# 64-row tiles for the transposes of q and k, and GpSimd's attention and routing work moved to VectorE and ScalarE

## The chip, the cores and the metric

The kernel runs on one core of one Trainium2 chip. The metric is the device time of one execution in microseconds (us), the median of several runs; lower is better. A core has a matrix engine (PE, with its weight loads listed as PEld), a vector engine (DVE), a scalar engine (ACT), a general engine (GpSimd, listed as POOL) and a queue engine (SP) that issues most of the transfers.

## The reference

Three blocks in a row. The first is a recurrence over time for 4 batches, 8 heads, 768 steps and a head size of 48:

```python
scale = np.minimum(mag, 0.999) / (mag + 1e-06)   # mag = |a_re + i a_im|
for t in range(S):
    new_re = ar * S_re - ai * S_im
    new_im = ar * S_im + ai * S_re
    S_re, S_im = (new_re + kv, new_im)           # kv = outer product of k[t], v[t]
    y[:, :, t] = np.einsum('bhd,bhde->bhe', q[:, :, t], S_re)
```

Its output, 3072 tokens of 384 values, goes through `((x @ w_a) * (x @ w_b)) @ w_out` with 1536 inner columns. The last block sends each token whose skip score `x @ w_skip` is positive to the one of 8 experts with the highest gate value, `relu(x @ w1[e]) @ w2[e]` weighted by the gate's softmax value, and adds the result to the token.

## The kernel before

**Units and groups.** The recurrence is computed in chunks of 128 time steps as a kind of attention. A unit is one chunk of one batch, with all 8 heads side by side in 384 columns; there are 24 units, and two make a group of 256 tokens, 12 groups (`g`). Per unit, `att_exp` makes the magnitudes: logarithms of the decay, a sum over time by a matmul with a triangle (`l2`, with a high and a low part `lh`, `ll` from the fifth unit on), exponentials `t1` and `t2`, and the products `q = q * t1` (line 332) and `k = k * t2` (line 333). The last row of `t1` is turned into a column by a copy `et` of 32 partitions (line 327) and a small transfer. `att_trig` makes the phases: an arctangent, a sum over time (`tp`), rounding (`t3`, line 362), a cosine `t4` and a sine `ts`; the products of q and k with them are `qr` and `kr` (lines 381 and 383), with 96 columns per head.

**The matmuls of a unit** are in `att_pe`. `turned` transposes q and k head by head against the identity (lines 425 and 430), four heads per PSUM bank (`pq`, `pk`), and ACT copies each bank to `tq` or `tk` of 512 columns. `scores` multiplies them in strips of 32 columns of the array (`pcs`, line 444; the first six units do it in whole tiles, `pc`); DVE masks the scores into `sc` (line 453). `delta` (`ds`, line 403) and `y` (line 482) follow, in strips as well. Then `xt` takes over y in a high part on ACT and a low one on DVE (lines 493 and 494), and `new_state` carries the state on (lines 413 and 415).

**The second block**, `moe1`, runs 12 steps per group: 18 matmuls `ab` (lines 615 to 617), an ACT copy `asb`, a DVE product with it (line 623) that frees the bank, `gh` on ACT, `gl` on DVE, and 6 matmuls `op` two steps later (lines 599 to 601). **Routing** of a finished group is `route`: maxima, a one-hot row `oh` from `eq` (lines 681 and 688), running counts `ohs` (line 701), positions, comparisons `sl` of an index row with them (line 738), and a matmul into a table. The experts come after all groups.

**Order.** While group g goes through `moe1`, the attention of group g + 1 and the routing of group g - 2 are worked in between. The order of each engine's instructions up to about the sixth unit is written out by hand (`ORDER`); after that the compiler's list planner chooses it from its own simulated times. Instructions of one engine run in the planned order. PSUM has eight banks: two each for `ab`, `op`, `at` (shared by `l2`, `tp`, `pq`, `pk`, `ds`, `y` and the routing's matmuls, in rotation) and `at2`, which from the seventh unit on hold the scores (`env.pc`). `PLACE` lists units whose operations go to another engine than the usual one.

Of the kernel before, what the change touches and what calls it, by code (L numbers as in the profile page):

```python
# [16 lines left out]
ALU = mybir.AluOpType  # L17
# [62 lines left out]
GF = 5  # L80
WO = DM + 10
# [37 lines left out]
def kern(tc, q, k, v, a_re, a_im, w_a, w_b, w_out, w_skip, w_gate, w1, w2, out):  # L119
# [3 lines left out]
    with st:  # L123
# [167 lines left out]
        def att_exp(i):  # L291
# [23 lines left out]
            if i < SPL:  # L315
                pe.matmul(l2[:, :W], tri, t1, start=True, stop=True)
            else:
                hi, lo = parts(i, "l", ("t3", "t4"))
                copy(on("lh", i, act), hi, t1)
                on("ll", i, pool).tensor_tensor(out=lo, in0=t1, in1=hi, op=ALU.subtract)  # L320
                cumsum(l2, hi, lo)
# [5 lines left out]
            pool.tensor_copy(et[96:], t1[96:].rearrange("p (h d) -> p d h", d=D))  # L327
# [4 lines left out]
            on("q", i, pool).tensor_tensor(out=d["q"], in0=d["q"], in1=t1, op=ALU.mult)  # L332
# [4 lines left out]
        def att_trig(i):  # L337
# [24 lines left out]
            dve.scalar_tensor_tensor(out=t3, in0=t3, scalar=MAGIC, in1=tp[:, :W], op0=ALU.subtract, op1=ALU.subtract)  # L362
# [11 lines left out]
            for nm in ("q", "k"):  # L374
# [8 lines left out]
                ins = e.tensor_tensor(out=r[:, :, 1], in0=src, in1=ts.rearrange("t (h d) -> t h d", d=D), op=ALU.mult)  # L383
                if e is dve:
                    mark((nm + "r", i), ins)
# [4 lines left out]
        def att_pe(i):  # L390
# [3 lines left out]
            sc, qT = [], []  # L394
# [14 lines left out]
            def new_state(ds):  # L409
                s3 = stt.rearrange("p (h e) -> p h e", e=VP)[:, :, :D]  # L410
                d3 = ds[:96, :W].rearrange("p (h e) -> p h e", e=D)
                if c > 0:
                    dve.tensor_tensor(out=s3, in0=s3, in1=d3, op=ALU.add)
                    d3 = s3
                dve.tensor_tensor(out=s3, in0=d3, in1=ee[:, :, None].to_broadcast([96, H, D]), op=ALU.mult)
# [6 lines left out]
            def turned(hh):  # L422
                pq = at(f"pq{i}_{hh}")
                for j in range(4):
                    pe.transpose(pq[:96, j * P : (j + 1) * P], qr[:, 4 * hh + j].rearrange("t x d -> t (x d)"), ident)  # L425
                tq = ew.tile([96, 512], F32, tag="tq", name=f"tq{i}_{hh}", bufs=2)
                mark(("tq", i, hh), copy(on("tq", 2 * i + hh, act), tq, pq[:96]))
                pk = at(f"pk{i}_{hh}")
                for j in range(4):
                    pe.transpose(pk[:96, j * P : (j + 1) * P], kr[:, 4 * hh + j].rearrange("t x d -> t (x d)"), ident)  # L430
                tk = ew.tile([96, 512], F32, tag="tk", name=f"tk{i}_{hh}", bufs=2)
                done = mark(("tk", i, hh), copy(on("tk", 2 * i + hh, act), tk, pk[:96])).ins
                qT.append(tq)
                return tq, tk, done

            def scores(hh, tq, tk, done, last):
                pc = at(f"pc{i}_{hh}") if i < CAUSAL else env.pc[hh]
                for j in range(4):
                    if i < CAUSAL:
                        last = pe.matmul(pc[:, j * P : (j + 1) * P], tk[:, j * P : (j + 1) * P], tq[:, j * P : (j + 1) * P], start=True, stop=True).ins  # L440
                        continue
                    for x in (0, 1, 2, 3) if j % 2 == 0 else (3, 2, 1, 0):
                        y0, p0 = j * P + STRIP * (x if j % 2 == 0 else 3 - x), STRIP * x
                        ins = pe.matmul(pc[p0 : p0 + STRIP, y0 : (j + 1) * P], tk[:, y0 : y0 + STRIP], tq[:, y0 : (j + 1) * P], start=True, stop=True).ins  # L444
# [13 lines left out]
            halves = []  # L458
            for hh in range(2):
                halves.append(turned(hh))  # L460
                if i < CAUSAL:
                    last, msk = scores(hh, *halves[hh], last)
            if i >= CAUSAL:
                for hh in range(2):
                    last, msk = scores(hh, *halves[hh][:2], halves[1][2], last)
# [12 lines left out]
            for s_, inter, h, col, begin, end in (t for row in zip(*strips) for t in row):  # L478
                p0, hh, j = STRIP * (s_ % 4), h // 4, h % 4
                o = y[p0 : p0 + STRIP, s_ // 4 * P : (s_ // 4 + 1) * P]  # L480
                l, r = (stt, qT[hh][:, j * P : (j + 1) * P]) if inter else (vt, sc[hh][:, j])
# [12 lines left out]
            dve.tensor_tensor(out=xt[:, :, 1, us], in0=y3, in1=xt[:, :, 0, us], op=ALU.subtract)  # L494
# [173 lines left out]
        def route(g):  # L668
# [31 lines left out]
            for t in range(2):  # L700
                pool.tensor_tensor(out=ohs, in0=ohs, in1=oh[:, t], op=ALU.add)
# [13 lines left out]
            sls = compare((2 * g, 2 * g + 1), dve if last else pool)  # L715
# [18 lines left out]
        def compare(tiles, eng=pool):  # L734
# [494 lines left out]
```

## Time and profile before

| | |
|---|---|
| median of 3 runs | 845.05 us (844.81 to 845.98) |
| the profiled execution | 847.09 us, of which the span from first to last instruction is 845.4 us |
| mean granted TensorE clock in it | 0.997 |
| busy: PE, DVE, ACT, POOL | 799.0, 559.8, 459.7, 235.0 us |

Busy time is the union of an engine's instructions. Matmuls are pipelined, so the duration of one is longer than its distance to the next, and a busy PE is not one at its peak. Idle time of an engine that sets nothing costs nothing.

### The profile page before, as it was taken

The numbers are of one execution on the slowest core, as the hardware profiler recorded it, in microseconds if no ns is written. First come the engines' busy times: TensorE is split into PE (matmuls) and PEld (weight loads), VectorE is DVE, ScalarE is ACT, GpSimd is POOL, SyncE is SP. The second block draws the span as 40 slices with busy tenths as digits, with TensorE's granted clock in tenths as the row PEclk, the third lists the DMA queues.
The fourth block names the chain that finished last, engine by engine and source line by source line (L and its number), as shares of the span: only waits on it lengthen the run. The fifth ranks groups of instructions, "written<-read, shape, count | busy, mean of one in ns | idle before, by whom it ended". The sixth has DMA issues, their size and how long they took to land.

```text
span 845.4 us, 21833 instructions
## 1 busy us (share of the span) xinstructions
PE 799.0 (95%) x8827; PEld 768.4 (91%) x8827; DVE 559.8 (66%) x1339; ACT 459.7 (54%) x949; POOL 235.0 (28%) x274
## 2 busy tenths in 40 slices
PE   1899999999999999999999999999999999999995
PEld 0589899999999999999999999999999989999995
DVE  7899888695884867738677386673736547555541
ACT  6798655364564655636547365473634325555540
POOL 3131353320311113102130031300304125757650
PEclk9999999999999999999999999999999999999998
DMA  9995223152341522313222132111103239776600
GB/s 256 243 299 131 52 58 77 22 126 38 83 90 25 114 53 72 63 26 85 45 72 58 30 84 45 50 38 28 32 2 115 74 118 347 222 223 199 194 22 23
DMA packets 180959, 83.15 MB, mean 98 GB/s; under 512 B 152084, under 2 KB 168026, under 8 KB 180848
## 3 DMA queue, kind: packets, MB, share of 16 engines
q1 hardware_dynamic: 178800, 76.26, 35.2%
q0 software_dynamic: 2048, 5.40, 1.8%
q8 instruction: 71, 1.16, 0.6%
q14 instruction: 40, 0.33, 0.1%
HBM read 69.84 MB, written 12.61 MB: 98 GB/s over the span
## 4 chain that ended last, share of the span: by engine, by line
PE 80%; DVE 10%; issue 4%; ACT 3%; POOL 1%; DMA 1%; POOLq 0%; ACTq 0%; DVEq 0%
PE ab L615 10%; PE ab L616 10%; PE ab L617 10%; PE op L600 5%; PE op L601 5%; PE op L599 5%; PE y L482 4%; PE eh L901 3%; PE eh L902 3%; PE eh L904 3%; PE eo L918 3%; PE eo L919 3%; PE eo L920 3%; PE pcs L444 2%; PE pq L425 2%
## 5 line engine op out<-in xcount | busy, mean ns | idle before, releaser
L615 PE MATMUL ab<-xt,wa 128*128 128x256 f32 x432 | 124.5, 289 | 7.5 <-DVE asb L623 7.3
L615 PE MATMUL ab<-xt,wb 128*128 128x256 f32 x432 | 123.3, 285 | 0.1
L616 PE MATMUL ab<-xt,wb 128*128 128x256 f32 x432 | 122.8, 284 | 0.0
L617 PE MATMUL ab<-xt,wa 128*128 128x256 f32 x432 | 122.5, 284 | 0.0
L616 PE MATMUL ab<-xt,wa 128*128 128x256 f32 x432 | 122.4, 283 | 0.0
L617 PE MATMUL ab<-xt,wb 128*128 128x256 f32 x432 | 122.2, 283 | 0.0
L623 DVE TENSOR_TENSOR asb<-ab,asb 128x256 f32<-128x256 f32 x144 | 60.3, 419 | 73.0 <-ACT asb L272 71.8
L600 PE MATMUL op<-wo,gh 128*128 128x394 f32 x288 | 99.7, 346 | 1.7 <-POOL wo L512 1.7
L601 PE MATMUL op<-wo,gh 128*128 128x394 f32 x288 | 99.6, 346 | 0.0
L599 PE MATMUL op<-wo,gl 128*128 128x394 f32 x288 | 98.6, 346 | 0.0
L272 ACT ACTIVATE asb<-ab 128x256 f32<-128x256 f32 x139 | 53.0, 381 | 70.1 <-PE ab L617 64.1
L615 PEld LDWEIGHTS ab<-xt,wa 128*128 128x128 f32 x432 | 81.3, 189 | 9.9 <-DVE asb L623 9.1
L272 ACT ACTIVATE gh<-asb 128x256 fp32r<-128x256 f32 x132 | 54.7, 415 | 61.2 <-DVE asb L623 61.2
L616 PEld LDWEIGHTS ab<-xt,wb 128*128 128x128 f32 x432 | 81.4, 188 | 1.3 <-issue 1.2
L617 PEld LDWEIGHTS ab<-xt,wb 128*128 128x128 f32 x432 | 81.3, 188 | 1.1 <-issue 1.0
L615 PEld LDWEIGHTS ab<-xt,wb 128*128 128x128 f32 x432 | 81.4, 188 | 0.9 <-issue 0.6
L616 PEld LDWEIGHTS ab<-xt,wa 128*128 128x128 f32 x432 | 81.4, 189 | 0.7 <-issue 0.4
L617 PEld LDWEIGHTS ab<-xt,wa 128*128 128x128 f32 x432 | 81.3, 188 | 0.0
L627 DVE TENSOR_TENSOR gl<-asb,gh 128x256 fp32r<-128x256 f32 x131 | 60.7, 465 | 30.9 <-ACT gh L272 30.2
L869 POOL TENSOR_TENSOR wq<-stg,wq 128x768 fp32r<-128x768 f32 x32 | 59.5, 1862 | 49.1 <-issue 24.8
L320 POOL TENSOR_TENSOR ll<-t,lh 128x384 fp32r<-128x384 f32 x19 | 19.9, 1050 | 163.1 <-ACT lh L272 118.0
L908 DVE SCALAR_TENSOR_TENSOR hl<-eh,hh 128x256 fp32r<-128x256 f32 x64 | 27.1, 424 | 52.2 <-ACT hh L907 52.1
(257 smaller groups left out, 2123.2 us busy)
## 6 DMA issues: line engine op xcount, KB each, us to landing
stg<-in_moe_w_dram SPq DMA_DIRECT2D x28, 768.0 KB
rawa<-in_moe_w_a_dram SPq DMA_DIRECT2D x6, 768.0 KB
re<-in_a_re_dram SPq DMA_DIRECT2D x24, 192.0 KB
rawb<-in_moe_w_b_dram SPq DMA_DIRECT2D x6, 768.0 KB
q<-in_q_dram SPq DMA_DIRECT2D x24, 192.0 KB
k<-in_k_dram SPq DMA_DIRECT2D x24, 192.0 KB
rawo<-in_moe_w_out_dram SPq DMA_DIRECT2D x6, 768.0 KB
xd<-xr SPq DMA_DIRECT2D x24, 192.0 KB
```

Source lines behind the costliest of these rows:

```text
L272: return act.activation(out=out, in_=in_, func=AF.Copy) if e is act else e.tensor_copy(out, in_)
L482: ins = pe.matmul(o, l[:, col : col + STRIP], r, start=begin, stop=end).ins
L599: pe.matmul(o, gl[:, ts], wh, start=f == 0, stop=False)
L600: pe.matmul(o, gh[:, ts], wl, start=False, stop=False)
L601: i = pe.matmul(o, gh[:, ts], wh, start=False, stop=f == NF - 1)
L615: pe.matmul(o, wl, xt[:, c, 0], start=c == 0, stop=False)
L616: pe.matmul(o, wh, xt[:, c, 1], start=False, stop=False)
L617: pe.matmul(o, wh, xt[:, c, 0], start=False, stop=c == NCC - 1)
L623: dve.tensor_tensor(out=asb, in0=ab[:, 256:], in1=asb, op=ALU.mult)
L627: on("gl", n).tensor_tensor(out=gl, in0=asb, in1=gh, op=ALU.subtract)
L869: lo.tensor_tensor(out=o[:, 1], in0=t, in1=o[:, 0], op=ALU.subtract)
L908: vm = dve.scalar_tensor_tensor(out=gl, in0=o, scalar=0.0, in1=gh, op0=ALU.max, op1=ALU.subtract)
```

## The change

For units 6 to 23 the transposes are cut in halves of 64 rows: each head gives two, one from rows 64 to 127 and one from rows 0 to 63, that take the matching 64 x 64 block of the identity and write 64 columns each, into two banks. All 16 of q and then all 16 of k are tied into one order. q's halves go to two `at` banks, k's to the two score banks. `tq` and `tk` are now single tiles of 1024 columns with one buffer, and each of the four copies writes every second 64 columns. The first transposes wait by hand-made dependencies: for the last product of kr, and in even units for `t3` of the next unit, in odd ones for the low part of `xt` and the first state update of the unit before.

From the ninth unit on (`PORT = 8`), `ll` and the product `q * t1` go to DVE and the copy `et` to ACT; in all groups `ohs` and `sl` go to DVE. In `ORDER` only names of `tq` and `tk` change.

```diff
+PORT = 8
+ROWS = 64
...
-                on("ll", i, pool).tensor_tensor(out=lo, in0=t1, in1=hi, op=ALU.subtract)
+                on("ll", i, pool if i < PORT else dve).tensor_tensor(out=lo, in0=t1, in1=hi, op=ALU.subtract)
...
-            pool.tensor_copy(et[96:], t1[96:].rearrange("p (h d) -> p d h", d=D))
+            copy(pool if i < PORT else act, et[96:], t1[96:].rearrange("p (h d) -> p d h", d=D))
...
-            on("q", i, pool).tensor_tensor(out=d["q"], in0=d["q"], in1=t1, op=ALU.mult)
+            on("q", i, pool if i < PORT else dve).tensor_tensor(out=d["q"], in0=d["q"], in1=t1, op=ALU.mult)
...
-            def turned(hh):
-                pq = at(f"pq{i}_{hh}")
+            tq, tk = (ew.tile([96, H * P], F32, tag=nm, name=f"{nm}{i}", bufs=1) for nm in ("tq", "tk"))
...
+            def turned_rows(nm, dst, r, banks, last):
+                for h in range(H):
+                    for x, p_ in ((1, banks[1]), (0, banks[0])):
+                        rows = slice(ROWS * x, ROWS * (x + 1))
+                        ins = pe.transpose(p_[:96, h * ROWS : (h + 1) * ROWS], r[rows, h].rearrange("t x d -> t (x d)"), ident[rows, rows]).ins
+                        for w in [last] if last else [d["krw"], marks["t3", i + 1]] if i % 2 == 0 else [d["krw"]] + env.free:
+                            after(ins, w, mybir.DependencyClass.NoSync if last else mybir.DependencyClass.Sync)
+                        last = ins
+                d3 = dst.rearrange("e (h t) -> e h t", t=P)
+                for x, p_ in enumerate(banks):
+                    cp = copy(act if x == 0 else act, d3[:, :, ROWS * x : ROWS * (x + 1)], p_[:96].rearrange("e (h t) -> e h t", t=ROWS))
+                return last, cp.ins
...
+            if i < CAUSAL:
                 for hh in range(2):
-                    last, msk = scores(hh, *halves[hh][:2], halves[1][2], last)
+                    turned("q", tq, qr, hh)
+                    turned("k", tk, kr, hh)
+                    last, msk = scores(hh, None, last)
+            else:
+                last, _ = turned_rows("q", tq, qr, [at(f"pq{i}_{x}") for x in range(2)], None)
+                _, done = turned_rows("k", tk, kr, env.pc, last)
+                last = None
+                for hh in range(2):
+                    last, msk = scores(hh, done, last)
...
-            dve.tensor_tensor(out=xt[:, :, 1, us], in0=y3, in1=xt[:, :, 0, us], op=ALU.subtract)
+            env.free = [dve.tensor_tensor(out=xt[:, :, 1, us], in0=y3, in1=xt[:, :, 0, us], op=ALU.subtract).ins]
...
-                pool.tensor_tensor(out=ohs, in0=ohs, in1=oh[:, t], op=ALU.add)
+                dve.tensor_tensor(out=ohs, in0=ohs, in1=oh[:, t], op=ALU.add)
...
-            sls = compare((2 * g, 2 * g + 1), dve if last else pool)
+            sls = compare((2 * g, 2 * g + 1))
...
-        def compare(tiles, eng=pool):
+        def compare(tiles, eng=dve):
```

## Rows read from the trace of the kernel before

**Rows 1.** The page's busy times: us, share of the span, instructions.
```profile
PE 799.0 (95%) x8827; PEld 768.4 (91%) x8827; DVE 559.8 (66%) x1339; ACT 459.7 (54%) x949; POOL 235.0 (28%) x274
```
**Rows 2.** PE's waits, 217 to 640 us: total us, times, longest us.
```profile
PE ab L615 <- DVE asb L623: 6.6, 7, 1.0
```
**Rows 3.** Timeline of PE around a quartet: start, duration in us.
```profile
397.35 0.60 PE L425 MATMUL pq<-ident,qr 128*96 128x128 f32 x4
397.71 0.36 PE L617 MATMUL ab<-xt,wa 128*128 128x256 f32 x1
397.91 0.28 PE L615 MATMUL ab<-xt,wb 128*128 128x256 f32 x1
```
**Rows 4.** Timeline of PE after the y of a unit.
```profile
412.41 0.39 PE L616 MATMUL ab<-xt,wa 128*128 128x256 f32 x1
412.63 0.28 PE L617 MATMUL ab<-xt,wa 128*128 128x256 f32 x1
412.75 0.28 PE L615 MATMUL ab<-xt,wb 128*128 128x256 f32 x1
```
**Rows 5.** Groups of PE, 217 to 539 us: busy us, mean ns, idle before.
```profile
L425 PE MATMUL pq<-ident,qr 128*96 128x128 f32 x96 | 14.4, 272 | 0.0
```
**Rows 6.** Timeline of weight loads, six in a row.
```profile
52.72 0.76 PEld L561 LDWEIGHTS wt<-wg,wtt 128*128 128x128 f32 x6
```
**Rows 7.** Groups of weight loads, whole span.
```profile
L430 PEld LDWEIGHTS pk<-ident,kr 128*96 128x96 f32 x192 | 22.1, 127 | 1.4 <-PE pq L425 0.5
...
L561 PEld LDWEIGHTS wt<-wg,wtt 128*128 128x128 f32 x72 | 9.1, 191 | 1.2 <-ACT wtt L272 1.2
...
L885 PEld LDWEIGHTS xgp<-ident,xg 128*128 128x128 f32 x48 | 5.6, 139 | 0.4 <-DMA xg<-xd,giu 0.4
```
**Rows 8.** Timeline of PE in the ds of a unit.
```profile
409.87 0.26 PE L403 MATMUL ds<-v,kr 128*32 128x48 f32 x6
409.95 0.26 PE L403 MATMUL ds<-u,kr 128*32 128x48 f32 x6
```
**Rows 9.** Groups of DVE by shape, 217 to 540 us.
```profile
L333 DVE TENSOR_TENSOR k<-k,t 128x384 f32<-128x384 f32 x13 | 14.7, 1167 | 11.6 <-ACT t L223 11.6
...
L381 DVE TENSOR_TENSOR kr<-k,t 128x384 f32<-128x384 f32 x12 | 6.6, 549 | 0.0
```
**Rows 10.** Groups of ACT, 217 to 539 us.
```profile
L272 ACT ACTIVATE asb<-ab 128x256 f32<-128x256 f32 x72 | 27.6, 384 | 30.1 <-PE ab L617 27.2 <-PE pt L750 1.6
...
L272 ACT ACTIVATE tq<-pq 96x512 f32<-96x512 f32 x24 | 14.2, 590 | 9.5 <-PE pq L425 9.5
```
**Rows 11.** Groups of POOL, 217 to 539 us.
```profile
L332 POOL TENSOR_TENSOR q<-q,t 128x384 f32<-128x384 f32 x12 | 15.1, 1271 | 0.5
L738 POOL TENSOR_SCALAR sl<-iota,rt_pos 128x256 bf16<-128x256 bf16 x12 | 12.7, 1063 | 0.0
L320 POOL TENSOR_TENSOR ll<-t,lh 128x384 fp32r<-128x384 f32 x12 | 12.6, 1048 | 130.7 <-ACT lh L272 95.7 <-DVE asb L623 35.0
L327 POOL COPY et<-t 32x384 f32<-32x384 f32 x12 | 10.5, 877 | 24.3 <-ACT t L223 23.9
```
**Rows 12.** One tile's instructions (sl): ns min/median/max, first and last start.
```profile
L738 DVE TENSOR_SCALAR sl<-iota,rt_pos x2: 274/298/323, 686.1 to 686.4; 128x256 bf16<-128x256 bf16 x2
```
**Rows 13.** Timeline of all engines at a group's start.
```profile
275.87 0.21 DVE L681 SCALAR_TENSOR_TENSOR eq<-lg,m,desc 128x8 f32<-128x8 f32 x1
...
275.94 0.39 ACT L272 ACTIVATE asb<-ab 128x256 f32<-128x256 f32 x1
...
276.07 0.88 POOL L327 COPY et<-t 32x384 f32<-32x384 f32 x1
...
276.18 0.80 DVE L681 SCALAR_TENSOR_TENSOR eq<-lg,m,desc 128x8 f32<-128x8 f32 x1
...
277.75 0.41 DVE L623 TENSOR_TENSOR asb<-ab,asb 128x256 f32<-128x256 f32 x1
...
278.22 0.39 PE L615 MATMUL ab<-xt,wa 128*128 128x256 f32 x1 [1.00 <-DVE asb L623]
```

More of the change, by code (lines that the diff above doesn't have):

```diff
@@ L361, in att_trig @@
                 dve.tensor_scalar(out=t3, in0=tp[:, :W], scalar1=MAGIC, scalar2=None, op0=ALU.add)
-            dve.scalar_tensor_tensor(out=t3, in0=t3, scalar=MAGIC, in1=tp[:, :W], op0=ALU.subtract, op1=ALU.subtract)
+            marks["t3", i] = dve.scalar_tensor_tensor(out=t3, in0=t3, scalar=MAGIC, in1=tp[:, :W], op0=ALU.subtract, op1=ALU.subtract).ins
             if c + 1 < NCH:
@@ L383, in att_trig @@
                 ins = e.tensor_tensor(out=r[:, :, 1], in0=src, in1=ts.rearrange("t (h d) -> t h d", d=D), op=ALU.mult)
+                d[nm + "rw"] = ins.ins
                 if e is dve:
@@ L393, in att_pe @@
             qr, kr, vt, ee = d["qr"], d["kr"], d["v"], d["ee"]
-            sc, qT = [], []
+            sc = []
             stt = state[b]
@@ L412, in new_state @@
                 if c > 0:
-                    dve.tensor_tensor(out=s3, in0=s3, in1=d3, op=ALU.add)
+                    env.free.append(dve.tensor_tensor(out=s3, in0=s3, in1=d3, op=ALU.add).ins)
                     d3 = s3
@@ L420, in att_pe, with turned @@
             last = None
-            def turned(hh):
-                pq = at(f"pq{i}_{hh}")
+            tq, tk = (ew.tile([96, H * P], F32, tag=nm, name=f"{nm}{i}", bufs=1) for nm in ("tq", "tk"))
+            def turned(nm, dst, r, hh):
+                p_ = at(f"p{nm}{i}_{hh}")
                 for j in range(4):
[L425 to L434, printed above, removed]
@@ L436, in scores @@
-            def scores(hh, tq, tk, done, last):
+                    pe.transpose(p_[:96, j * P : (j + 1) * P], r[:, 4 * hh + j].rearrange("t x d -> t (x d)"), ident)
+                mark(("t" + nm, i, hh), copy(on("t" + nm, 2 * i + hh, act), dst[:, 4 * P * hh : 4 * P * (hh + 1)], p_[:96]))
+            def turned_rows(nm, dst, r, banks, last):
[10 more added lines that the diff above has]
+                return last, cp.ins
@@ L437, in scores @@
+            def scores(hh, done, last):
                 pc = at(f"pc{i}_{hh}") if i < CAUSAL else env.pc[hh]
                 for j in range(4):
+                    tks, tqs = (x[:, (4 * hh + j) * P : (4 * hh + j + 1) * P] for x in (tk, tq))
                     if i < CAUSAL:
-                        last = pe.matmul(pc[:, j * P : (j + 1) * P], tk[:, j * P : (j + 1) * P], tq[:, j * P : (j + 1) * P], start=True, stop=True).ins
+                        last = pe.matmul(pc[:, j * P : (j + 1) * P], tks, tqs, start=True, stop=True).ins
@@ L441, in scores @@
                         continue
                     for x in (0, 1, 2, 3) if j % 2 == 0 else (3, 2, 1, 0):
-                        y0, p0 = j * P + STRIP * (x if j % 2 == 0 else 3 - x), STRIP * x
-                        ins = pe.matmul(pc[p0 : p0 + STRIP, y0 : (j + 1) * P], tk[:, y0 : y0 + STRIP], tq[:, y0 : (j + 1) * P], start=True, stop=True).ins
+                        y0, p0 = STRIP * (x if j % 2 == 0 else 3 - x), STRIP * x
+                        ins = pe.matmul(pc[p0 : p0 + STRIP, j * P + y0 : (j + 1) * P], tks[:, y0 : y0 + STRIP], tqs[:, y0:], start=True, stop=True).ins
@@ L456, in scores @@
                 return last, msk
[L458 to L463, printed above, removed]
-                for hh in range(2):
-                    last, msk = scores(hh, *halves[hh][:2], halves[1][2], last)
+            if i < CAUSAL:
+                for hh in range(2):
+                    turned("q", tq, qr, hh)
[7 more added lines that the diff above has]
+                    last, msk = scores(hh, done, last)
             pcs = last
@@ L480, in att_pe @@
                 o = y[p0 : p0 + STRIP, s_ // 4 * P : (s_ // 4 + 1) * P]
-                l, r = (stt, qT[hh][:, j * P : (j + 1) * P]) if inter else (vt, sc[hh][:, j])
+                l, r = (stt, tq[:, h * P : (h + 1) * P]) if inter else (vt, sc[hh][:, j])
                 ins = pe.matmul(o, l[:, col : col + STRIP], r, start=begin, stop=end).ins
```

4 rows, old and new, of the table ORDER are left out of this document.

## The prediction

> **What bounds the kernel now.** I read the page first. PE is busy for 95% of the span and the next engine, DVE, for 66% [rows 1]; so what the array executes is the time, unless a wait on another engine ends last. The list of PE's waits comes next. Only one of them recurs: the first matmul of an `ab` step waits for DVE's `asb` product, 7 times and 6.6 us in all between 217 and 640 us, with 1.0 us the longest [rows 2]. Little else there is not the array's own work. A change in this stage is therefore worth what it takes off PE's stream, plus at most those stalls.
>
> Then the timeline of PE around one quartet of transposes. Four of them start at 397.35 and the next `ab` matmuls at 397.71 and 397.91 [rows 3]. Neighbouring `ab` matmuls are 0.12 us apart [rows 4], so a quartet costs 0.56 - 0.12 = 0.44 us. One transpose follows another after (0.60 - 0.27) / 3 = 0.11 us, although each lasts 0.27 [rows 3, 5]: they are pipelined, and it is the distance that counts. The 96 of q in this stretch (12 units by 8) have one form [rows 5], and k has as many.
>
> **Part 1, the transposes.** It removes, in each of 18 units, 4 quartets: 4 x 0.44 = 1.76 us, 31.7 us in all. It puts in their place 32 transposes per unit of 64 rows, each with 96 columns of weights and 64 columns of the identity streamed, alternately in the upper and the lower half of the array's rows and in two banks. No row shows a tile of 64 rows, so I bound it from both sides.
>
> The low end: the two halves run at once, with loads hidden. Streaming 64 columns instead of 128 takes 0.11 x 64/128 = 0.055 us, and 16 pairs take 0.88 us. The high end: every load takes its turn. Six loads of 128 columns that have almost nothing to hide behind (10 columns streamed) span 0.76 us [rows 6] with 0.19 for one [rows 7], so they are 0.114 us apart; for 96 columns that is 0.086, and 32 of them take 2.7 us, 21 us more than now over all units with the edges below. In between, the loads of transposes are lighter than that row: 127 ns for 96 columns against 139 for 128, and 191 for a load that isn't a transpose's [rows 7]. That is 12 ns for 32 columns, so some 36 ns of a transpose's load depend on its size.
>
> I take the low end. Its nearest row is the kernel's other tiled work, `ds`: three strips of 32 columns side by side, with 48 columns streamed. Six of them start every 0.08 us [rows 8], 14 ns each, so three share 0.042 us. At 0.11 us per 128 columns one alone would stream for 0.041 us. So three tiles of the array stream at once, and their three loads are hidden as well. Those are column strips, not row halves; that is the step I trust least.
>
> A change of tile shape has a price too. After the tiled `y` matmuls the first two `ab` are 0.22 us apart instead of 0.12 [rows 4]; I take these 0.10 us for each edge, 0.20 for a visit. The transposes of a unit can go in one block, since q has two `at` banks and k has the two score banks, which nobody else holds then; before, the third quartet had to wait for a copy to empty its bank. So one visit per unit: 0.88 + 0.20 = 1.08 us against 1.76, a gain of 0.68 x 18 = 12.2 us. If the planner splits the block into two visits, 3.6 us of this go.
>
> The Trainium skill speaks against this part (TensorE: Matmul & The Clock Gate, Part 3: Packing small matmuls, The mechanism): a weight load overlaps matmuls in flight only where its row group differs. By that rule each half would load and then stream, and the sum would be the rival of exposed loads below. This trace disagrees as far as it goes: the loads of [rows 7] last longer than the 0.11 us between transposes that use all rows, so they do overlap in the same rows.
>
> The new waits. A unit's transposes now wait for both halves of kr; those of an even unit also for t3 of its odd neighbour, and those of an odd one for the evacuation of its predecessor's y and ds. The banks' rotation asked for the last one before already. What is queued behind on PE is the `ab` and `op` work of the other group, and the planner places it around the block; DVE's part of kr is 0.55 us [rows 9]. I cost this at nothing; that cover gone, a block late by one such DVE operation in each unit would cost 0.55 x 18 = 10 us.
>
> The copies stay 4 per unit of 0.59 us on ACT [rows 10], with the same 512 columns. But q's and k's come in one burst of 2.4 us instead of two pairs, and an `asb` copy may stand behind it for 1.2 us more. ACT sits idle before `asb` copies for 30.1 us in six groups [rows 10], and two `ab` banks give cover, so the near end is 0; the far end is 1.2 x 18 = 21 us. I take 1.5 us.
>
> **Part 2, GpSimd's work.** Per group of two units it leaves GpSimd: two q products of 1.27 us, two ll of 1.05, two comparisons `sl` of 1.06, two copies et of 0.88 [rows 11], and two small additions `ohs`. DVE gets q and ll at 0.55 each, the price of a like product with GpSimd idle [rows 9], and `sl` at 0.30 [rows 12]; with `ohs` at some 0.15 (an estimate from the 0.21 of `eq` [rows 13]), 3.1 us. It gets back what it loses to GpSimd now: k takes 1.17 us instead of 0.55 [rows 9], 1.2 us per group, and `eq`, on 8 columns, 0.80 beside et where its twin took 0.21 [rows 13], 0.6 us. So DVE's sum rises by about 1.3 us per group, 10 us in all, against 285 us in which it is idle [rows 1]. ACT gets two et copies: no row has 32 partitions there; between 0.38 for 256 columns and 0.59 for 512 [rows 10] I take 0.5, so 1.0 us.
>
> All this is off PE's path except at the recurring stall. In one of the groups the `asb` copy starts at 275.94 and is done after 0.39 us; DVE's product, which frees the bank, starts only at 277.75, because `eq` sat beside et until 276.98 and the routing's next steps followed; PE resumes at 278.22 [rows 13]. Without GpSimd `eq` is 0.6 us earlier, but `ohs` and `sl` (0.9 us in all) and ACT's et copies may stand ahead of `asb`. All seven stalls of [rows 2] lie in groups that the change reaches. Ends: all of it gone, -6.6 us; ACT's 1.0 us ahead each time, +7. I take 0.4 us each, -3 us.
>
> **Sum.** -12.2 + 1.5 - 3 = -13.7 us. The profiled execution took 847.09 us for a span of 845.4, so 1.7 lie around the span, and it is 2.0 above the median of 845.05; the terms are differences inside the span, so I take them off the median: 831.4 us.
>
> **Rivals.**
> *Exposed loads.* Each half loads (0.036) and then streams (0.055): 16 x 0.091 + 0.20 = 1.66 us, a gain of only 1.8 us; with the other terms 841.7. If just the loads take turns (0.072 a pair), 1.35 us and 836.2. For it: no row of a tile with half the rows. Against: `ds` [rows 8].
> *The halves take turns* (the change then doesn't do what it says). 32 x 0.055 + 0.20 = 1.96 us, 0.20 more per unit, +3.6 us, with the other terms 847.2; with loads exposed as well, 868. The place is the block of 32. It decides from a distance between transposes of 0.049 us by itself ((1.76 - 0.20) / 32), and of 0.051 with the other terms. For it: the trace has column strips only.
> *The moved work lengthens the stall.* Et copies stand ahead of `asb` at 7 boundaries: +7 in place of -3, 841.4. For it: [rows 13] show DVE full there. Against: GpSimd's drag on `eq` and k is of the same size.
> *All stalls vanish*: -6.6 in place of -3, and no burst: 826.3.
>
> **How the numbers follow.** Chances: forecast 0.60 (827 to 836), all stalls gone 0.08, loads taking turns or exposed 0.13, moved work in the way 0.07, halves taking turns 0.12. The range leaves out the last and a little on either side: 824 to 844. Within 0.2% (1.7 us, about what a measurement of this kernel can tell from no change) lie the tails of the exposed loads, of the moved work and part of the halves' turns, 0.09; slower 0.11; faster 0.80.
>
> **What would show it.** In the profile after: transposes in pairs with some 0.055 us from pair to pair, and PE's busy sum lower; if the distance between single transposes is over 0.05 us, part 1 is wrong. One block per unit, with 0.1 us lost at each edge. `k` and `eq` at 0.55 and 0.2 us, GpSimd nearly empty until the experts. PE's waits for `asb` under 5 us; if they are above 7, or new waits stand before transposes or `pcs`, part 2 or the burst was costed wrongly. A new planned order could also move waits that I don't see.

## The result and the profile after

The changed kernel takes 837.12 us (median of 4 runs, 834.49 to 838.37) against 845.32 (4 runs, 844.81 to 845.98) for the kernel before: a ratio of 0.9896 [0.9882, 0.9910], or 8.2 us. The forecast was 831.4 with a range of 824 to 844. The profiled execution took 836.47 us for a span of 834.7, 10.7 us less than the span of 845.4 before. (That execution of before, 847.09 us, lay 1.8 us above this median and the one of the changed kernel 0.65 below its own, which is why spans differ by more than medians.)

The page of the changed kernel, the line of busy times that answers to [rows 1]:

```profile
PE 791.7 (95%) x9115; PEld 756.0 (91%) x9115; DVE 550.6 (66%) x1417; ACT 467.7 (56%) x965; POOL 152.9 (18%) x180
```

PE is as full as before, but with 7.3 us less work. POOL has lost 82 us; DVE has taken the moved work and is still 9 us less busy than before. Line numbers are higher by 2 to 14 now: the transposes are L437, `ab` L629 to L631, `y` L496, the product with `asb` L637, the masks `sc` L464.

The timeline of PE around the block of transposes of one unit (start, duration in us, form, count), which answers to [rows 3] and [rows 4]:

```profile
394.88 0.28 PE L631 MATMUL ab<-xt,wa 128*128 128x256 f32 x1
395.10 0.65 PE L437 MATMUL pq<-ident,qr 64*96 64x64 f32 x16
395.58 0.61 PE L437 MATMUL pcs<-ident,kr 64*96 64x64 f32 x16
396.12 0.39 PE L629 MATMUL ab<-xt,wb 128*128 128x256 f32 x1
396.35 0.28 PE L630 MATMUL ab<-xt,wb 128*128 128x256 f32 x1
396.47 0.28 PE L631 MATMUL ab<-xt,wb 128*128 128x256 f32 x1
```

All 32 stand in one block. From the `ab` before to the second `ab` behind it 396.35 - 394.88 = 1.47 us pass, and two ordinary `ab` distances of 0.12 come off: the block costs 1.23 us. The starts of the 18 blocks give a mean of 1.225, against 4 x 0.44 = 1.76 for the quartets. That is 0.53 us per unit, 9.6 us in all. From pair to pair it is 0.056 us. The rest of a block, 1.225 - 16 x 0.056 = 0.33 us, lies at its ends: the first transpose comes 0.21 us after the last `ab` instead of 0.12; the second pair comes 0.096 after the first (0.108 where the loads are wider, experiment 5), which I put down to the first loads, with nothing of their kind ahead to hide behind; the next `ab` starts 0.146 after the last transpose instead of 0.056; and the one after that 0.224 later instead of 0.12.

PE's waits (total us, times, longest us) of the same kernel, whole span, those of this stage; they answer to [rows 2]:

```profile
PE y L496 <- DVE sc L464: 3.3, 3, 1.8
PE ab L629 <- DVE asb L637: 1.6, 3, 0.6
PE pt L764 <- DVE sl L752: 0.8, 1, 0.8
PE y L496 <- issue: 0.4, 1, 0.4
```

The same view of the kernel before, whole span:

```profile
PE ab L615 <- DVE asb L623: 7.3, 8, 1.0
...
PE y L482 <- issue: 1.9, 3, 0.8
...
PE y L482 <- DVE sc L453: 0.9, 1, 0.9
```

These sum to 10.1 us, the four of the changed kernel to 6.1. The stall that I looked at has nearly gone. A new one stands first: `y` waits for the mask of the scores, once for 1.8 us. The timelines of PE and, in the second fence, of DVE just there:

```profile
188.58 1.33 PE L455 MATMUL pcs<-tq,tk 96*32 96x128 f32 x64
...
192.89 0.30 PE L496 MATMUL y<-sc,v 128*32 128x128 f32 x1 [1.78 <-DVE sc L464]
```

```profile
188.08 0.56 DVE L280 TENSOR_SCALAR_CACHE_REDUCE chk<-chk 128x384 f32<-128x384 f32 x1 [1.15 <-DMA chk<-in_a_re_dram]
...
190.35 0.55 DVE L324 TENSOR_TENSOR im<-im,t 128x384 f32<-128x384 f32 x1
190.82 0.42 DVE L637 TENSOR_TENSOR asb<-ab,asb 128x256 f32<-128x256 f32 x1
191.69 0.55 DVE L283 TENSOR_REDUCE immax<-chk 128x1 f32<-128x384 f32 x1 [0.45 <-DMA chk<-in_a_im_dram]
192.16 0.68 DVE L464 TENSOR_TENSOR sc<-pcs,keep 128x512 int32<-128x512 int32 x1
```

The scores (`pcs`) were through at 189.9 us. The new order puts the late range test of another unit, an operation on `chk` and one on `immax` that check its input and that nothing needs before the end of the kernel, ahead of the mask. The second one waits 0.45 us for its transfer and takes 0.55. The first had waited 1.15 us already, with the products behind it pushed back; `asb` and other work fill the rest. So the mask that PE needs starts 2.3 us after its input was there. What follows on PE is the second loss. Here are three windows of the changed kernel (stretch and its us; busy us and count of PE, PEld, DVE, ACT, POOL; PEclk, the granted clock as a share of 2.4 GHz; DMA share, GB/s):

```profile
192.00:193.00 1.00, 0.11 (x2) 0.11 (x4) 1.00 (x3) 0.00 (x0) 0.00 (x0) 1.00 0.36 66
193.60:197.00 3.40, 3.40 (x23) 3.28 (x16) 2.14 (x5) 1.35 (x3) 0.00 (x0) 0.50 0.29 58
197.00:201.00 4.00, 4.00 (x57) 3.67 (x56) 2.65 (x7) 1.18 (x3) 0.15 (x1) 1.00 0.20 36
```

After PE's 1.78 us without a matmul the granted clock falls to 0.50, 1.2 GHz, for 3.4 us. `ab` matmuls start 0.213 us apart there instead of 0.118. The 15 distances from 193.72 to 197.06 us take 3.34 us; at the full clock they would take 0.22 + 14 x 0.118 = 1.87. So the fall costs 1.5 us on top of the stall. The spread of the runs goes with it, though only one of them has a trace: the one with a mean granted clock of 0.997, which is that of before, took 834.49 us, those with 0.994 took 836.47 and 837.77, and the one with 0.992 took 838.37.

The groups of DVE (217 to 540 us) and, in the second fence, of ACT (217 to 530 us) that answer to [rows 9 to 13] (busy us, mean ns, idle before):

```profile
L334 DVE TENSOR_TENSOR q<-q,t 128x384 f32<-128x384 f32 x14 | 7.8, 555 | 3.1 <-ACT t L225 2.4
L335 DVE TENSOR_TENSOR k<-k,t 128x384 f32<-128x384 f32 x14 | 7.7, 552 | 0.0
L322 DVE TENSOR_TENSOR ll<-t,lh 128x384 fp32r<-128x384 f32 x12 | 6.7, 556 | 1.8 <-ACT lh L274 1.6
L752 DVE TENSOR_SCALAR sl<-iota,rt_pos 128x256 bf16<-128x256 bf16 x14 | 3.3, 277 | 0.0
L695 DVE SCALAR_TENSOR_TENSOR eq<-lg,m,desc 128x8 f32<-128x8 f32 x14 | 2.6, 217 | 0.0
L715 DVE TENSOR_TENSOR ohs<-ohs,rt_oh 128x8 bf16<-128x8 bf16 x14 | 2.1, 150 | 0.0
```

```profile
L274 ACT ACTIVATE asb<-ab 128x256 f32<-128x256 f32 x73 | 27.7, 380 | 32.2 <-PE ab L631 31.4 <-DVE rt_r L719 0.5
L274 ACT ACTIVATE et<-t 32x384 f32<-32x384 f32 x12 | 10.8, 897 | 2.6 <-DMA ee<-et 2.4
```

DVE's operations cost what was forecast: `k` 0.55 instead of 1.17, `eq` 0.22 throughout, `q` and `ll` 0.55, `sl` 0.28, `ohs` 0.15. The copy `et` on ACT takes 0.90 us, not the 0.5 that I took, and as long as on POOL.

**The balance of the profiled spans.** Blocks -9.6, listed stalls -4.0, the clock +1.5: -12.1. Measured: -10.7. Some 1.4 us stay without a row. It is a balance of one execution of each kernel; the medians differ by 8.2.

### The profile page after: what moved, and what is told of

Read it like the earlier page. It is cut to its first block, busy times and chain, and to the rows that moved or that the text cites. A ratio compares the mean times of both kernels' runs of the same rounds, so it can differ in the third digit from the quotient of the medians.

```text
span 834.7 us, 22309 instructions
## 1 busy us (share of the span) xinstructions
PE 791.7 (95%) x9115; PEld 756.0 (91%) x9115; DVE 550.6 (66%) x1417; ACT 467.7 (56%) x965; POOL 152.9 (18%) x180
## 4 chain that ended last, share of the span: by engine, by line
PE 75%; DVE 8%; ACT 6%; DMA 5%; issue 3%; POOL 1%; SPq 1%; POOLq 0%; ACTq 0%; DVEq 0%
PE ab L629 10%; PE ab L630 10%; PE ab L631 10%; PE op L613 5%; PE op L615 5%; PE op L614 5%; PE y L496 5%; PE eh L915 3%; PE eh L916 3%; PE eo L932 3%; PE eh L918 3%; PE eo L934 3%; PE eo L933 3%; ACT t L225 2%; PE pcs L455 2%
## 5 line engine op out<-in xcount | busy, mean ns | idle before, releaser
L629 PE MATMUL ab<-xt,wa 128*128 128x256 f32 x432 | 124.2, 288 | 1.8 <-DVE asb L637 1.6
L629 PE MATMUL ab<-xt,wb 128*128 128x256 f32 x432 | 123.2, 285 | 0.1
L631 PE MATMUL ab<-xt,wb 128*128 128x256 f32 x432 | 122.4, 283 | 0.0
L631 PE MATMUL ab<-xt,wa 128*128 128x256 f32 x432 | 122.1, 283 | 0.0
L637 DVE TENSOR_TENSOR asb<-ab,asb 128x256 f32<-128x256 f32 x144 | 60.3, 419 | 83.2 <-ACT asb L274 82.6
L629 PEld LDWEIGHTS ab<-xt,wa 128*128 128x128 f32 x432 | 81.7, 189 | 4.3 <-DVE asb L637 2.4
L629 PEld LDWEIGHTS ab<-xt,wb 128*128 128x128 f32 x432 | 81.8, 189 | 1.0 <-issue 0.4
L631 PEld LDWEIGHTS ab<-xt,wb 128*128 128x128 f32 x432 | 81.5, 189 | 1.1 <-issue 1.0
L631 PEld LDWEIGHTS ab<-xt,wa 128*128 128x128 f32 x432 | 81.8, 189 | 0.1
L641 DVE TENSOR_TENSOR gl<-asb,gh 128x256 fp32r<-128x256 f32 x131 | 58.3, 447 | 31.4 <-ACT gh L274 30.3
L259 POOL MEMSET v<- 128x64 f32 x24 | 3.5, 150 | 400.3 <-PE y L496 337.4
L921 ACT ACTIVATE hh<-eh 128x256 fp32r<-128x256 f32 x64 | 24.6, 385 | 66.9 <-PE eh L918 66.9
```

The source lines that it names most:

```text
L629: pe.matmul(o, wl, xt[:, c, 0], start=c == 0, stop=False)
L631: pe.matmul(o, wh, xt[:, c, 0], start=False, stop=c == NCC - 1)
L637: dve.tensor_tensor(out=asb, in0=ab[:, 256:], in1=asb, op=ALU.mult)
L641: on("gl", n).tensor_tensor(out=gl, in0=asb, in1=gh, op=ALU.subtract)
```

## The experiments

Ratios are to the kernel before, measured beside it on the same chip: one chip for experiments 1 to 4, one for 5 to 8, one for 9 to 12. The planner makes a new order for every variant, so each edit also moves operations that it doesn't name.

**1. The tiles alone** (`tiles_only`): part 2 undone.

```diff
-PORT = 8
+PORT = 24
...
-                dve.tensor_tensor(out=ohs, in0=ohs, in1=oh[:, t], op=ALU.add)
+                pool.tensor_tensor(out=ohs, in0=ohs, in1=oh[:, t], op=ALU.add)
...
-            sls = compare((2 * g, 2 * g + 1))
+            sls = compare((2 * g, 2 * g + 1), dve if last else pool)
...
-        def compare(tiles, eng=dve):
+        def compare(tiles, eng=pool):
```

> Part 1 alone: the 64-row blocks, with all of GpSimd's work left on GpSimd. Theory A (the blocks take 1.22 us per unit instead of 1.76, and this is most of the gain): 18 x 0.53 = 9.6 us off, so 834 to 838 us, blocks of 1.22 us as in the changed kernel, and the waits of PE for asb at the group starts stay at 6 to 7 us. Theory B (GpSimd's departure makes the gain, the blocks only look shorter because the edges move): 842 to 846 us.

839.41 us (838.02 to 842.13), ratio 0.9907 [0.9881, 0.9933]; theory A's range was missed by 1.4 us. Its blocks cost 1.227 us, as in the full change. So part 1 by itself accounts for the result as far as this interval tells. But the stall for `asb`, which I had expected to stay, went too, and masks came still later. PE's waits of this kernel, and in the second fence two of its windows (columns as above):

```profile
PE y L496 <- DVE sc L464: 5.9, 4, 2.3
PE ab L629 <- DVE asb L637: 1.0, 2, 0.6
```

```profile
195.00:200.00 5.00, 5.00 (x57) 4.24 (x53) 3.30 (x8) 1.29 (x3) 0.47 (x2) 0.73 0.29 57
250.00:255.00 5.00, 5.00 (x57) 4.56 (x57) 3.51 (x7) 0.88 (x2) 1.01 (x2) 0.77 0.29 56
```

The granted clock falls twice here, behind waits for masks of 1.8 and 2.3 us. The late masks and the falls therefore come with part 1's new order, not with the work moved off GpSimd.

**2. GpSimd's work alone** (`port_only`): the kernel before with part 2.

```diff
+PORT = 8
...
-                on("ll", i, pool).tensor_tensor(out=lo, in0=t1, in1=hi, op=ALU.subtract)
+                on("ll", i, pool if i < PORT else dve).tensor_tensor(out=lo, in0=t1, in1=hi, op=ALU.subtract)
...
-            pool.tensor_copy(et[96:], t1[96:].rearrange("p (h d) -> p d h", d=D))
+            copy(pool if i < PORT else act, et[96:], t1[96:].rearrange("p (h d) -> p d h", d=D))
...
-            on("q", i, pool).tensor_tensor(out=d["q"], in0=d["q"], in1=t1, op=ALU.mult)
+            on("q", i, pool if i < PORT else dve).tensor_tensor(out=d["q"], in0=d["q"], in1=t1, op=ALU.mult)
...
-        def compare(tiles, eng=pool):
+        def compare(tiles, eng=dve):
```

> Part 2 alone: the transposes as before in quartets of 128 rows, q, ll, et, ohs and sl off GpSimd. Theory A: PE's waits for asb fall from 7.3 to under 3 us, other waits may rise by 1 to 2, so 839 to 843 us. Theory B (this part makes the whole gain): 836 to 839 us. Theory C (the moved work costs what it gives): 844 to 847 us.

845.20 us (844.49 to 846.46, 12 runs), ratio 0.9981 [0.9967, 0.9995]: about 1.6 us, in the range of theory C. The recurring stall shrinks but doesn't go, where theory A wanted it under 3 us. PE's wait in this kernel:

```profile
PE ab L616 <- DVE asb L624: 4.5, 10, 1.0
```

**3. The masks ahead of the late tests** (`masks_first`): the changed kernel with one more dependency, which holds each late range test until the second mask of the unit at hand is done.

```diff
-                test(i, t)
+                after(test(i, t).ins, marks["sc", i + 6, 1])
```

> The changed kernel with the late range tests of the first six units placed on DVE behind the masks of the unit at hand; nothing is left out. Theory D (PE's wait of 1.8 us for a mask at 191 us makes the granted clock fall for 3.4 us afterwards, in some runs, and this costs the changed kernel 2 to 3 us of its median): that wait is 0.5 us or less, mean clock 0.997 in nearly all runs, 833.5 to 835.5 us with a spread under 1.5 us. Theory E (the clock falls by itself or after another wait): spread and clock as in the changed kernel, 0.992 to 0.997, and 836 to 838 us.

833.29 us (832.85 to 834.68), ratio 0.9838 [0.9812, 0.9863], and a mean clock of 0.996 or 0.997 in all five runs. DVE's timeline and, in the second fence, PE's waits in this kernel:

```profile
189.80 0.68 DVE L464 TENSOR_TENSOR sc<-pcs,keep 128x512 int32<-128x512 int32 x1
...
191.39 0.68 DVE L464 TENSOR_TENSOR sc<-pcs,keep 128x512 int32<-128x512 int32 x1
191.99 0.54 DVE L280 TENSOR_SCALAR_CACHE_REDUCE chk<-chk 128x384 f32<-128x384 f32 x1
```

```profile
PE ab L629 <- DVE asb L637: 3.0, 7, 0.6
PE y L496 <- DVE sc L464: 0.6, 3, 0.2
```

The mask starts 2.4 us earlier than in the changed kernel, the wait for masks is 0.6 us in all, and no fall of the clock is left in this stage. Theory D held in its mechanism; its numbers did not quite: the late tests cost the changed kernel 4 to 5 us, stall and clock together, and not 2 to 3, the time is 0.2 us under its range and the spread 1.8 us. The balance of this span: blocks -9.6, stalls 10.1 to 4.4 (the two above and 0.8 for `sl`), so -5.7, sum -15.3; measured 831.3 - 845.4 = -14.1. Some 1.2 us stay without a row, as 1.4 did above.

**4. The halves one after the other** (`halves_apart`): the changed kernel with the two loops exchanged, so that eight transposes of one half are followed by eight of the other.

```diff
-                for h in range(H):
-                    for x, p_ in ((1, banks[1]), (0, banks[0])):
+                for x, p_ in ((1, banks[1]), (0, banks[0])):
+                    for h in range(H):
```

> The changed kernel with all heads of rows 64 to 127 ahead of all heads of rows 0 to 63 instead of alternating; nothing is left out. Theory F (neighbours in different halves run at once; alone each streams its 64 columns): 0.055 us from one transpose to the next, a block of 32 x 0.055 + 0.31 = 2.07 us, 0.85 x 18 = 15 us more than the changed kernel, 850 to 854 us. Theory G (a transpose of 64 rows is shorter by itself, pairing plays no part): the blocks stay at 1.22 us, 836 to 838 us.

840.95 us (838.39 to 841.31), ratio 0.9926 [0.9897, 0.9955]. A block costs 1.60 us, between what the two theories gave. PE's timeline shows why:

```profile
290.07 0.75 PE L437 MATMUL pq<-ident,qr 64*96 64x64 f32 x13
290.61 0.26 PE L437 MATMUL pcs<-ident,kr 64*96 64x64 f32 x1
290.66 0.22 PE L437 MATMUL pq<-ident,qr 64*96 64x64 f32 x1
```

k's first transposes, in the upper half, start between the last of q's in the lower one, although they stand behind them in the order. Within one half they stay 0.056 us apart. So the halves do run at once wherever transposes of both can be started, and PE overlaps part of the runs even in this order. Putting them in pairs is worth (1.60 - 1.225) x 18 = 6.8 us of PE's time. The run itself is only 3.8 us longer than that of the changed kernel: here `y` waits 1.4 us for masks instead of 3.3, and the clock does not fall.

**5. Wider loads, in pairs** (`wide_pairs`): the kernel of 3 with 128 columns of weights per transpose, the last head excepted. The upper 32 rows of each result aren't used.

```diff
-                        ins = pe.transpose(p_[:96, h * ROWS : (h + 1) * ROWS], r[rows, h].rearrange("t x d -> t (x d)"), ident[rows, rows]).ins
+                        wide = P if h + 1 < H else 96
+                        ins = pe.transpose(p_[:wide, h * ROWS : (h + 1) * ROWS], r.rearrange("t h x d -> t (h x d)")[rows, 96 * h : 96 * h + wide], ident[rows, rows]).ins
```

> As masks_first, but each 64-row transpose (but the last head's) loads 128 columns of weights instead of 96 and still streams 64; the extra rows of its output are not used, nothing is left out. Theory H (a pair takes 0.057 us because each half streams its 64 columns, loads hidden): the distance from pair to pair stays at 0.057 us and the block at 1.22 us. Theory I (the loads set it, two per pair): with a third more columns the distance becomes 0.076 us and the block 1.5 us.

833.79 us in one run, beside 845.52 for before. A block costs 1.33 us, 0.062 us from pair to pair instead of 0.056. The loads of q's transposes in the changed kernel, from the view of one tile's instructions in a stretch (ns min/median/max, first and last start):

```profile
L437 PEld LDWEIGHTS pq<-ident,qr x48: 119/123/126, 240.1 to 292.1; 64*96 64x96 f32 x48
```

and in this one:

```profile
L438 PEld LDWEIGHTS pq<-ident,qr x48: 121/138/142, 235.9 to 288.0; 64*128 64x128 f32 x42, 64*96 64x96 f32 x6
```

**6. Wider loads, halves apart** (`wide_apart`): the same with the loops of experiment 4.

```diff
-                for h in range(H):
-                    for x, p_ in ((1, banks[1]), (0, banks[0])):
+                for x, p_ in ((1, banks[1]), (0, banks[0])):
+                    for h in range(H):
```

> The same wide loads with the halves apart, where one transpose followed another after 0.040 us. Theory H (streaming sets it): 0.040 us again and a block of 1.60 us. Theory I (the load of 96 columns sets it when one half works alone): 0.053 us and a block of 2.0 us. One of the two rows can also change and the other not: then pairs and single halves have different limits.

840.02 us in one run; a block costs 1.75 us (1.60 with 96 columns), single transposes 0.063 apart. In both orders a third more columns loaded adds 0.006 to 0.007 us to the distance, and neither theory's number came: it is neither unchanged nor a third longer. With the same 96 columns loaded, 128 columns streamed took 0.11 us in the kernel before and 64 take 0.056 here. So at 96 columns what is streamed sets the distance and the load hides behind it, in the same rows; that at 128 the load begins to show is the likeliest reading, from one run of each order. The runs with pairs and without differ by 6.2 us, with masks on time in both; 18 x (1.75 - 1.33) is 7.6.

**7. The routing back on GpSimd** (`route_back`): the kernel of 3 with `ohs` and `sl` on GpSimd, by the last three edits of experiment 1.

> masks_first with ohs and sl back on GpSimd, q, ll and et off it. Theory J (part 2 gives little because ohs and sl on DVE stand in front of asb, where PE still waits 3.0 us, and 0.8 us for sl itself): PE's waits for asb under 1.5 us, none for sl, 830 to 832 us. Theory K (GpSimd's reading is what delays DVE there, whatever its work): the waits for asb at 5 us or more, 835 to 837 us.

831.67 us (830.13 to 832.80), ratio 0.9834 [0.9820, 0.9847]. The wait for `asb` falls from 3.0 to 0.4 us, as theory J said; PE still waits 0.6 us for `sl`.

**8. The copy et back on GpSimd** (`et_back`): the kernel of 3 with one edit.

```diff
-            copy(pool if i < PORT else act, et[96:], t1[96:].rearrange("p (h d) -> p d h", d=D))
+            copy(pool, et[96:], t1[96:].rearrange("p (h d) -> p d h", d=D))
```

> masks_first with the copies et back on GpSimd, all else off it. They take 0.90 us each on ACT, more than the 0.5 that I had put, and two of them stand ahead of asb copies at a group's start. Theory L (they are part of why asb is late): waits for asb under 2 us, 831 to 833 us. Theory K (GpSimd's reading delays DVE's eq beside et): waits of 4 us or more, 834 to 836 us. Neither: 833.3 us as in masks_first.

831.96 us (829.75 to 833.24), ratio 0.9833 [0.9817, 0.9849]. Its `ab` waits 1.2 us for `asb`, in seven waits of 0.2 at most. Three of its five runs have a mean clock of 0.992 or 0.993; in the profiled one the granted clock is at 0.50 from 40 to 45 us, in the first units, which this edit does not touch. The two runs with 0.996 and 0.997 took 829.75 and 830.72. Neither 7 nor 8 parts from 3 by more than its interval.

**9. The tiles alone, masks on time** (`tiles_masks`): experiment 1 with the edit of experiment 3.

```diff
-                test(i, t)
+                after(test(i, t).ins, marks["sc", i + 6, 1])
```

> Part 1 alone (all of GpSimd's work on GpSimd) with the late range tests behind the masks. Theory M (part 2 gives 2 to 4 us once the masks are on time, through the waits for asb): 835.5 to 838 us, PE's waits for asb 4 us or more or the waits for masks over 3 us. Theory N (part 2 gives nothing; tests behind the masks and the blocks are the whole gain): 831.5 to 834 us.

833.52 us (831.94 to 834.30), ratio 0.9846 [0.9828, 0.9864].

**10. The kernel of 3 once more** (`masks_again`), unchanged, on the same chip as 9, 11 and 12.

> masks_first once more, on the chip of this call, to compare with: 832.5 to 834.5 us, no fall of the clock before the end in most runs.

833.08 us (832.66 to 834.03), ratio 0.9845 [0.9829, 0.9862]. With the masks on time, the kernel with part 2 and the one without it (9) take the same time: part 2 as a whole brings nothing that can be measured here.

**11. The masks on time in the kernel before** (`before_masks`): the edit of experiment 3, with the tiles of 128 rows and all of GpSimd's work.

```diff
-                test(i, t)
+                after(test(i, t).ins, marks["sc", i + 6, 1])
```

> The kernel before with nothing but the late range tests placed behind the masks. Theory D (what they cost is a wait that the planned order of the changed kernel made worse): 0 to 1.5 us faster than before, 844 to 846 us. Theory P (the tests cost the kernel before as much, and the gain of masks_first isn't the changed kernel's alone): 841 to 843 us.

845.04 us (843.55 to 847.88, 12 runs), ratio 0.9984 [0.9970, 0.9997]: 1.3 us. The edit is worth little where masks weren't late, so what experiment 3 brings is a repair of what the changed order broke, not a gain of its own.

**12. Only q and ll leave GpSimd** (`q_ll_only`): the kernel of 3 with the edits of 7 and 8 together.

```diff
-            copy(pool if i < PORT else act, et[96:], t1[96:].rearrange("p (h d) -> p d h", d=D))
+            copy(pool, et[96:], t1[96:].rearrange("p (h d) -> p d h", d=D))
...
-        def compare(tiles, eng=dve):
+        def compare(tiles, eng=pool):
```

> masks_first with et, ohs and sl back on GpSimd; only q and ll leave it. Theory Q (each of the three moves back took away a wait of PE of its own: asb behind sl, asb behind et): 829 to 831 us, waits for asb and sl under 1.5 us together. Theory K (GpSimd beside eq delays asb again): waits for asb at 4 us or more, 833 to 836 us.

829.38 us (828.75 to 831.96), ratio 0.9799 [0.9782, 0.9815]: the fastest of all, 17 us under before and 3.7 under experiment 10. The starts of the copies `lg` (one pair per group of tokens, groups counted from 1 here) divide the stage; worked out from the traces, in us:

```
                 from group 2's lg to group 9's   from there to group 11's
before                     374.8                          101.5
changed kernel             365.5                          103.6
masks_again (10)           362.1                          103.7
tiles_masks (9)            364.5                          101.0
route_back (7)             363.1                          102.0
et_back (8)                361.2                          101.3
q_ll_only (12)             362.1                          100.4
```

Moving q and ll brings 2.4 us in the first stretch (9 against 12). Moving `et`, `ohs` and `sl` as well adds nothing there (10 against 12) and costs 3.3 us in the second. At its end DVE's timeline in kernel 10 shows

```profile
627.85 1.86 DVE L641 TENSOR_TENSOR gl<-asb,gh 128x256 fp32r<-128x256 f32 x1 [1.82 <-ACT gh L274]
629.64 1.78 DVE L715 TENSOR_TENSOR ohs<-ohs,rt_oh 128x8 bf16<-128x8 bf16 x1
```

and POOL's beside it

```profile
627.59 3.81 POOL L883 TENSOR_TENSOR wq<-stg,wq 128x768 fp32r<-128x768 f32 x2 [52.14 <-DMA stg<-in_moe_w_dram]
```

while in kernel 12 DVE's timeline shows

```profile
627.48 0.42 DVE L641 TENSOR_TENSOR gl<-asb,gh 128x256 fp32r<-128x256 f32 x1 [0.48 <-ACT gh L274]
```

and POOL's

```profile
628.38 0.20 POOL L715 TENSOR_TENSOR ohs<-ohs,rt_oh 128x8 bf16<-128x8 bf16 x1 [41.42 <-PE pp L711]
629.38 1.85 POOL L883 TENSOR_TENSOR wq<-stg,wq 128x768 fp32r<-128x768 f32 x1 [0.81 <-ACT wq L882]
```

GpSimd, idle for 52 us, starts on the experts' weights as soon as they land, and two operations of DVE that fall beside it take 1.8 us instead of 0.42 and 0.15; `sl` is late behind them and PE waits 0.8 us for it. With `ohs` and `sl` in its queue GpSimd does the weights between them, after that `gl`, which stays at 0.42. A later `rt_oh` takes 1.89 us beside the weights there, and no wait of PE follows. The place of an operation in the order decides this and not the engine of `ohs` and `sl` alone: kernel 8 has them on DVE too, GpSimd starts on the weights at 628.85 us, behind both, and its second stretch is 101.3. Either move back (7 or 8) takes most of the 3.3 us away. The rest of it wasn't taken apart, and the table has one profile of each kernel.

## Why the prediction was right or wrong

**Direction and range: right.** 837.12 lies in 824 to 844 and was given 0.80 as faster. It is 5.7 us above the likeliest time and 1.1 above the forecast's own 827 to 836. Of the 5.7 us, 3.0 lie in the terms (-13.7 against -10.7 between the spans): the blocks gave 2.6 less, the clock took 1.5 that had no price, the stalls gave 1.0 more. Another 2.5 are that the two profiled executions lie further apart than the medians, and 0.3 a higher median of the kernel before. The range was wide enough for all of it. That the 1.5 us for the copies and the 1.4 without a row are alike is luck as far as is known: no wait shows the copies' price.

**Part 1, the distance: right.** 0.055 us per pair was forecast, 0.056 came. `ds`, three strips at once [rows 8], was the right neighbour, though it has strips of columns and these are halves of rows. Both rivals here fall. *The halves take turns* would have shown 0.11 per pair; experiment 4 shows what a partial loss of the pairing costs: 6.8 us of PE's time. *Exposed loads* would have shown 0.091. The Trainium skill (TensorE: Matmul & The Clock Gate, Part 3: Packing small matmuls, The mechanism) lists that a load overlaps matmuls in flight only where its row group differs. This trace does not agree: transposes of one half follow one another every 0.056 us with loads that last 0.123 us, in the same rows. The same section of the Trainium skill also lets a load that goes to the background weight buffer pass matmuls in flight; no run here tells whether that is what happens. Experiments 5 and 6 show how far that hiding goes: at 128 columns the pair takes 0.062.

**Part 1, the edges: the mis-sized term.** I took 0.20 us per visit, from the second `ab` after `y` [rows 4]. It is 0.33: the entry (0.09) and the second distance behind the block (0.106) are those 0.20; left out were the first distance behind it (0.09) and the longer first distance between pairs (0.04). 0.13 x 18 = 2.3 us, and with the 0.001 per pair the gain is 9.6 us instead of 12.2. One block per unit held in all 18.

**The new waits: costed at nothing, and rightly at their own place.** No wait stands before the transposes in the list. The burst of copies, +1.5, has no row of its own: ACT is idle before `asb` for 32.2 us instead of 30.1 [rows 10], and `ab` waits less than before. The three waits of `ab` for `asb` that the list still has come at 432, 536 and 588 us, 20 us behind the start of the last block and right behind the routing's `pt`. Some 1.2 to 1.4 us without a row are left in both balances; that they are the burst isn't shown.

**The stalls: right in sum, wrong in place, and with a price that I hadn't counted.** -3 was forecast and -4.0 came in the listed waits. But `asb` fell by 5.7, not by 3, and a new wait for masks took 2.4 of it. I had named it only in the last sentence, as waits of a new planned order that I didn't see, without a price. Its mechanism is a late range test that waits for its transfers ahead of the mask on DVE. Experiment 3 takes it away and gives 833.3. The prediction had no term at all for what follows such a stall: the granted clock at 0.50 for 3.4 us, 1.5 us in the profiled run. The runs of the changed kernel with the highest mean clock (834.49 us) and with the lowest (838.37) lie 3.9 us apart.

**Part 2.** Each price of a moved operation on DVE was right, that of `et` on ACT was 0.4 us too low. The sum on DVE was wrong in sign: about 10 us more were forecast and its busy time fell by 9.2. The prediction let only `k` and `eq` get shorter without GpSimd beside them; others did too, such as `sk` (5.5 to 1.9 us over the kernel) and `rt_r` (11.6 to 8.5). The rival *the moved work lengthens the stall* did not occur at the boundaries of groups that I named: `asb` waits fell. That `asb` fell because of part 2 is wrong, however. It fell to 1.0 us in the tiles alone (1), and to 4.5 us only with part 2 alone (2). It is 3.7 us in experiment 11, where nothing is moved. The order, planned anew in every variant, moves this stall more than GpSimd's share of the work does. With the masks on time part 2 as a whole is worth nothing measurable (9 against 10): what q and ll bring, the moves of `et`, `ohs` and `sl` together take back (12). How they do so is shown for one place only, the two slow operations beside the experts' weights. I had looked for that price at [rows 13], in the middle of the stage, and it came at its end.

**What stays open.** Why the planner's order frees `asb` with the tiles was not traced to a single dependency, nor what most of the 3.3 us of experiment 12 are. The clock's early fall at 40 us in two profiles, before any edited step, is seen and not explained.

## What to carry to other kernels

A tiled matmul shape pays by its distance from start to start, but each visit has a price at both ends (0.33 us here, a quarter of the block), so count the ordinary neighbours on either side and gather the work in one block. When a planner makes a new order, follow every product that PE waits for and look at what stands ahead of it: work with no due time, waiting for a transfer, can hold the one product that is due, and one dependency repairs it. And move work off an engine piece by piece: two of the moves here (q and ll) paid and the other three together gave it back at another place and time.

## What the runs showed of the hardware that I had not expected

- Transposes in one half of the rows start before earlier ones of the other half that stand ahead of them in the order (290.61 against 290.66 us, experiment 4), so that a block of 32 in four runs of eight costs 1.60 us, neither 1.23 nor all in turn.
- A load of 96 columns that lasts 0.123 us hides behind 64 columns streamed every 0.056 us in the same rows; one of 128 columns, 0.138 us, gives 0.062.
- After PE stood for 1.78 us the granted clock fell to 1.2 GHz for 3.4 us; it fell behind stalls of 1.84 and 2.35 us in experiment 1 too, and in the kernel before and experiments 2, 3 and 4, with no stall of this stage above 1.45 us, it stayed at 2.4 GHz there. A stall alone doesn't settle it: no fall followed one of 1.52 us in experiment 1, nor the wait of some 1.65 us for `wo` at 90 us that every profile has.
- A copy of 32 partitions by 384 strided columns takes 0.90 us on ACT and 0.88 on GpSimd, so moving it makes it no shorter.
- GpSimd does not slow everything beside it: in kernel 10 `gl` and `ohs` took 1.86 and 1.78 us beside the conversion of the experts' weights, while `hl`, with one input in PSUM, took 0.42 in all 26 cases beside it as in the others.
